# Windowed attention and ELU feed-forward on one core: values loaded and split once per tile of 128 tokens for all heads

## The chip, the cores and the metric

The kernel runs on one core of a Trainium2 chip. The metric is device microseconds of one execution. TensorE does the matmuls (PE in the rows, its weight loads PEld), VectorE (DVE), ScalarE (ACT) and GpSimd (POOL) do the element work, and every transfer is issued by SyncE (SP). Each engine runs its own instructions strictly in program order.

## The reference

```python
# q, k, v: (4, 8, 768, 64) float32; n_sink = 4, window = 128
scores = np.matmul(q, k.transpose(0, 1, 3, 2)) / np.sqrt(64)
keep = (pos[None, :] < n_sink) | ((rel >= 0) & (rel < window))   # rel = query position - key position
a = softmax(np.where(keep, scores, -1e9))
x = np.matmul(a, v)                       # all heads beside each other: (3072, 512)
h = x @ w_in                              # 512 -> 2048
g = np.where(h > 0, h, np.exp(np.minimum(h, 0)) - 1)
out = g @ w_out                           # 2048 -> 512
```

## The kernel before

The 3072 tokens are 24 tiles of 128 (`NT` = 6 to a batch), in nine chunks of 2, 2, 2, 3, 3, 3, 3, 3 and 3 tiles (`SIZES`). For each chunk `attention(c)` makes the four blocks of x (one for each of `NP` = 4 head pairs), and `feed_forward` then goes over 16 blocks of the hidden width, two matmul groups each: `h` (L671, 12 matmuls) and `acc` (L692). The first two chunks take the 16 blocks in two halves (`PARTS`), since the weights, 32 pieces of 512 KB, are still coming in during that time. All operands are carried as a high and a low half (float16, or float32r for keys), made by ACT (the high half) and DVE or POOL (the low one).

A weight piece takes one load, one ACT instruction (L287), three on DVE (L289, L288, L290), then ACT (L436) and POOL (L437). An attention step for a tile and a head pair takes scores on PE (L567 in the first two chunks, L560 and L561 later), a masked minimum on DVE (L586), Exp on ACT (L588), a sum and a reciprocal (L592, L593), the probabilities' two halves (ACT L600, DVE L601), a transposing DMA on SP (L619), the value matmuls on PE (L630, and L635 for the four sink positions), and after a pair's last tile the copy out of PSUM into x (ACT L643, DVE L644). A block of the feed-forward takes ACT (L679, L684), DVE (L681, L682) and POOL (L685).

Values: for each chunk and each head pair, L527 loads a stretch of `vx` that holds, for every key tile of the chunk (the own tiles and the one before the first), 128 columns, and 128 more for the sink rows. ACT makes `vh` of it (L530), DVE `vl` (L531). Where a tile of the chunk lies two or more tiles into its batch, an ACT copy puts low halves of the sink rows into `vh` (L536, 8 partitions). Two raw buffers (`vs`) and two split ones (`vhl`) go round. So there are 36 loads and splits, 384, 512 or 640 columns wide, and 32 sink copies.

The order of all this is set by `Plan`: every step is a task with a cost and its inputs; PE tasks have fixed positions in two or three lines; the others are placed by list scheduling with due times, and the best of eight rounds is written out as each engine's program (`keep_order`). Ring buffers are constraints of the plan (`ring`). A change of tasks therefore changes the order elsewhere too.

Of the kernel before, what the change touches and what calls it, by code (L numbers as in the profile page):

```python
# [20 lines left out]
P = 128  # L21
# [31 lines left out]
RINGS = dict(kqs=2, kq=3, vs=2, vm=1, vhl=2, e=3, st=6, pq=3, pt=6, g=2, gh=3, x=7, wv=4, s=2, po=1, h=2, wu=2, sv=2, wps=1, raw=6)  # L53
# [20 lines left out]
NK_MAX = max(len(key_tiles(c)) for c in CHUNKS)  # L74
# [269 lines left out]
def fast_path(tc, ctx, first, kq, vx, wt, out, nw, flag):  # L344
# [15 lines left out]
    vh = rows("vh", [P, (NK_MAX + 1) * P], F16, RINGS["vhl"])  # L360
    vl = rows("vl", [P, (NK_MAX + 1) * P], F16, RINGS["vhl"])
# [108 lines left out]
    later = []  # L470

    def attention(c):
# [4 lines left out]
        vw = (nk + 1) * P  # L477
        far = any(g % NT >= 2 for g in ts)
# [38 lines left out]

        k = 0
        for p in range(NP):
            kqp = [split_keys(2 * p + e) for e in range(2 if c >= DUP else 1)]  # L520


            st = vs[slot("vs")]
            o = V_OFF[c, p]
            ld = None
            if (c, p) not in first["vs_"]:
                ld = add("SP", 0.4, lambda st=st, o=o: nc.sync.dma_start(st[:, :vw], vx[:, o : o + vw]), lat=dma_us(P * vw * 4))  # L527
            i = slot("vhl")
# [12 lines left out]
            for g in ts:  # L541
# [80 lines left out]
                def values(po=po, vhi=vhi, vlo=vlo, pt=pt, g=g, j=j, nb=nb, t=t):  # L622
# [394 lines left out]
```

## Time and profile before

| what | value |
|---|---|
| median of 3 runs | 658.06 us (657.52 to 658.17) |
| the profiled execution | 658.03 us, its span in the profile 656.2 us |
| PE busy | 611.0 us, 93% of the span |
| DVE, ACT, POOL busy | 458.4, 456.3, 338.8 us |
| mean granted TensorE clock | 0.984 of full speed |

The span is from the first to the last instruction; 1.8 us of the profiled execution lie around it. Busy time is time in which an engine has at least one instruction under way. Idle time of an engine costs only where something at the end waits for it.

### The profile page before, as it was taken

To read this page: it belongs to the slowest core of one execution; us is meant where nothing else is said; L and a number is where in the kernel's file an instruction comes from. 1 tells how busy PE (TensorE), PEld (TensorE's weight loads), DVE (VectorE), ACT (ScalarE), POOL (GpSimd) and SP (SyncE) were. 2 spreads that over 40 slices of the span, in tenths; PEclk is the share of its full clock that TensorE was granted. 3 is DMA by queue.
4 is the path that set the end of the run, shared out by engine and by line. 5 is a ranking of instruction groups with operands and counts; after the bars stand their busy time and mean duration, and the time that the engine had idled before them with its cause. 6 is when DMAs were issued, how large, how long until landed. Compare 5 with 4: busy or idle time off the path is not lost.

```text
span 656.2 us, 13438 instructions
## 1 busy us (share of the span) xinstructions
PE 611.0 (93%) x4449; PEld 370.1 (56%) x4449; DVE 458.4 (70%) x1251; ACT 456.3 (70%) x1340; POOL 338.8 (52%) x497
## 2 busy tenths in 40 slices
PE   3678699789999999999999999999999999999995
PEld 2444466457777665655555565565555556555552
DVE  6999999987677757757676877757686786533222
ACT  4988798887788878767677877766677776523221
POOL 0156878785565767544446656544446654212221
PEclk9998699999999999999999999999999999999998
DMA  7898976765647556445454666454655733211001
GB/s 266 202 284 231 267 213 209 246 171 154 140 126 155 159 151 129 117 116 158 100 147 114 186 135 164 79 157 136 125 140 122 213 91 90 61 42 44 1 0 54
DMA packets 130110, 93.41 MB, mean 142 GB/s; under 512 B 104432, under 2 KB 109552, under 8 KB 130032
## 3 DMA queue, kind: packets, MB, share of 16 engines
q1 hardware_dynamic: 130032, 92.47, 53.2%
q8 instruction: 37, 0.61, 0.4%
q14 instruction: 41, 0.34, 0.2%
HBM read 59.94 MB, written 7.34 MB: 103 GB/s over the span
## 4 chain that ended last, share of the span: by engine, by line
PE 81%; DVE 8%; DMA 3%; ACT 2%; issue 2%; POOL 2%; SPq 0%; DVEq 0%; POOLq 0%; ACTq 0%
PE h L671 35%; PE acc L692 34%; PE po L630 5%; PE s L560 3%; PE s L561 3%; DMA pt<-pq 2%; DVE wv L290 2%; DVE wu L288 1%; DVE pq L601 1%; PE s L567 1%; DVE wu L289 1%; DVE g L681 1%; POOL w L437 1%; ACT e L588 1%; ACT pq L600 1%
## 5 line engine op out<-in xcount | busy, mean ns | idle before, releaser
L671 PE MATMUL h<-x,w 128*128 128x384 f16 (+1 forms) x1728 | 278.1, 312 | 6.1 <-DVE g L682 6.1
L685 POOL TENSOR_TENSOR gl<-g,gh 128x384 f16<-128x384 f32 (+1 forms) x144 | 125.7, 874 | 195.8 <-ACT gh L684 163.2
L671 PEld LDWEIGHTS <-w 128*128 128x128 f16 x1728 | 166.5, 99 | 100.6 <-POOL w L437 4.0
L692 PE MATMUL acc<-w,gh 128*128 128x512 f16 x768 | 194.2, 382 | 0.7 <-ACT gh L684 0.7
L681 DVE TENSOR_SCALAR g<-g 128x384 f32<-128x384 f32 (+1 forms) x144 | 68.2, 474 | 109.1 <-ACT g L679 108.8
L679 ACT ACTIVATE g<-h 128x384 f32<-128x384 f32 (+1 forms) x144 | 65.0, 451 | 84.6 <-PE h L671 77.3
L601 DVE SCALAR_TENSOR_TENSOR pq<-e,st,pq 128x256 f16<-128x256 f32 (+1 forms) x192 | 104.7, 573 | 15.1 <-ACT pq L600 14.5
L692 PE MATMUL acc<-w,gl 128*128 128x512 f16 x384 | 109.3, 380 | 2.4 <-POOL gl L685 2.3
L692 PEld LDWEIGHTS <-gh 128*128 128x128 f16 x768 | 70.0, 98 | 70.9 <-ACT gh L684 1.2
L586 DVE CUSTOM_DVE_ANT_0 e<-s,m 128x264 f32<-128x264 f32 (+1 forms) x192 | 73.5, 404 | 41.5 <-PE s L561 38.0
L588 ACT ACTIVATE e<-e,st 128x264 f32<-128x264 f32 (+1 forms) x192 | 93.4, 487 | 11.5 <-DVE st L586 10.1
L684 ACT ACTIVATE gh<-g 128x384 f16<-128x384 f32 (+1 forms) x144 | 69.2, 481 | 44.6 <-DVE g L682 44.1
L600 ACT ACTIVATE pq<-e,st 128x256 f16<-128x256 f32 (+1 forms) x192 | 84.6, 479 | 10.0 <-DVE st L593 9.4
L507 POOL TENSOR_TENSOR kq<-kqs,kq 128x396 fp32r<-128x396 f32 (+1 forms) x56 | 68.5, 1224 | 37.8 <-ACT kq L503 37.2
L682 DVE SCALAR_TENSOR_TENSOR g<-g,h 128x384 f32<-128x384 f32 (+1 forms) x144 | 72.5, 503 | 1.3
L692 PEld LDWEIGHTS <-gl 128*128 128x128 f16 x384 | 37.5, 98 | 49.0 <-POOL gl L685 4.1
L503 ACT ACTIVATE kq<-kqs 128x780 fp32r<-128x780 f32 (+2 forms) x56 | 48.5, 878 | 17.1 <-PE s L561 15.5
L509 POOL TENSOR_TENSOR kq<-kqs,kq 64x384 fp32r<-64x384 f32 (+1 forms) x56 | 57.0, 1017 | 4.4
L560 PE MATMUL s<-kq 128*128 128x264 f32 x160 | 56.0, 367 | 3.0 <-DVE st L586 2.1
L437 POOL TENSOR_TENSOR w<-wv,w 128x512 f16<-128x512 f32 x32 | 38.8, 1218 | 37.2 <-DVE wu L289 16.6
L630 PE MATMUL po<-pt,vh 128*64 128x128 f16 x704 | 42.1, 230 | 7.7 <-DVE x L644 5.0
L561 PE MATMUL s<-kq 128*128 128x264 f32 x160 | 42.8, 284 | 0.0
(78 smaller groups left out, 620.7 us busy)
## 6 DMA issues: line engine op xcount, KB each, us to landing
raw<-in_wt_dram SPq DMA_DIRECT2D x32, 512.0 KB, 5.2
kqs<-in_kq_dram SPq DMA_DIRECT2D x24, 456.0 KB, 3.4
kqs<-in_kq_dram SPq DMA_DIRECT2D x24, 390.0 KB, 3.3
out_dram<-wv SPq DMA_DIRECT2D x24, 256.0 KB, 2.4
vs<-in_vx_dram SPq DMA_DIRECT2D x20, 256.0 KB, 2.8
vm<-in_vx_dram SPq DMA_DIRECT2D x6, 768.0 KB, 4.8
kqs<-in_kq_dram SPq DMA_DIRECT2D x12, 326.0 KB, 3.4
vs<-in_vx_dram SPq DMA_DIRECT2D x12, 320.0 KB, 3.1
```

What stands on the lines that cost most here:

```text
L560: nc.tensor.matmul(sp[:, :wd], q, hi[:, c0 : c0 + wd], start=True, stop=False)
L586: red = add("DVE", 0.13 + 0.00145 * wd, lambda ee=ee, me=me, sp=sps[e], m=m, wd=wd: nc.vector.tensor_tensor_reduce(ee, sp[:, :wd], m[:, :w ...
L588: ex = add("ACT", 0.48 + 0.00085 * wd, lambda ee=ee, me=me, rs=rs[:, e : e + 1]: nc.scalar.activation(ee, ee, AF.Exp, bias=me, scale=-1.0, ...
L600: a = add("ACT", act_us(nb * P, True), lambda src=src, hi=hi, re=re: nc.scalar.activation(hi, src, AF.Copy, scale=re), deps=[rr])
L601: b = add("DVE", dve_us(nb * P) + 0.1, lambda src=src, hi=hi, lo=lo, re=re: nc.vector.scalar_tensor_tensor(lo, src, re, hi, ALU.mult, ALU. ...
L630: nc.tensor.matmul(po[e * D : (e + 1) * D, oc], vv[:, vo : vo + D], pt[:, (2 * e + part) * nb + i, :], start=new, stop=last)
L671: nc.tensor.matmul(hp[:, :n], win[:, part, d, :], xx[:, :n], start=k == 0, stop=k == 3 * ND - 1)
L681: b = add("DVE", 0.1 + 0.0008 * n, lambda gf=gf: nc.vector.tensor_scalar(gf, gf, -1.0, G_SCALE, ALU.add, ALU.mult), deps=[a])
L682: b = add("DVE", dve_us(n), lambda gf=gf, hp=hp: nc.vector.scalar_tensor_tensor(gf, gf, 0.0, hp[:, :n], ALU.min, ALU.max), deps=[b])
L684: th = add("ACT", act_us(n), lambda gf=gf, gh=gh: nc.scalar.activation(gh[:, :n], gf, AF.Copy), deps=[b])
L685: tl = add("POOL", pool_us(n), lambda gl=gl, gf=gf, gh=gh: nc.gpsimd.tensor_tensor(gl[:, :n], gf, gh[:, :n], ALU.subtract), deps=[th])
L692: nc.tensor.matmul(acc[i], gg[:, i * P : (i + 1) * P], wout[:, part, :], start=f == f0 and k == 0, stop=f == f1 - 1 and k == 2)
```

## The change

Values are laid out in `vx` by token tile: 512 columns for all eight heads, 24 tiles, then one block of 512 columns of sink rows for each of the four batches. `vtile(g)` loads and splits a tile when the plan first asks for it, `sink_rows(b)` does so for a batch's sink rows, whose low halves DVE writes on partitions 64 to 95 in one instruction. All pairs, and the next chunk where it needs the tile again, use the same halves, from a ring of six (`vt`); sink rows have a ring of two (`sk`). There are 24 + 4 loads and 24 + 4 splits, all 512 columns wide, and no ACT copies of sink rows. The value matmuls read other addresses and are otherwise as before. The final range check of the values (L732 to L741) reads the same values in the new layout.

```diff
-RINGS = dict(kqs=2, kq=3, vs=2, vm=1, vhl=2, e=3, ...)
+RINGS = dict(kqs=2, kq=3, vs=2, vm=1, vt=6, sk=2, e=3, ...)
...
+        def vtile(g):
+            if g not in v_of:
+                st, i = vs[slot("vs")], slot("vt")
+                ld = None
+                if g not in first["vs_"]:
+                    ld = add("SP", 0.4, lambda: nc.sync.dma_start(st, vx[:, g * VT : (g + 1) * VT]), lat=dma_us(P * VT * 4))
+                hi, lo, users = vh[i], vl[i], []
+                va = add("ACT", act_us(VT), lambda: nc.scalar.activation(hi, st, AF.Copy, scale=V_SCALE), deps=[ld])
+                vb = add("DVE", 0.13 + 0.00108 * VT, lambda: nc.vector.scalar_tensor_tensor(lo, st, V_SCALE, hi, ALU.mult, ALU.subtract), deps=[va])
+                ring("vs", [ld or va], [va, vb])
+                ring("vt", [va], users)
+                v_of[g] = hi, lo, va, vb, users
+            return v_of[g]
+
+        def sink_rows(b):
+            if b not in sk_of:
+                st, sk, users = vs[slot("vs")], sks[slot("sk")], []
+                o = SINKS + b * VT
+                ld = add("SP", 0.4, lambda: nc.sync.dma_start(st, vx[:, o : o + VT]), lat=dma_us(P * VT * 4))
+                va = add("ACT", act_us(VT), lambda: nc.scalar.activation(sk, st, AF.Copy, scale=V_SCALE), deps=[ld])
+                vb = add("DVE", 0.13 + 0.00108 * VT, lambda: nc.vector.scalar_tensor_tensor(sk[64:96, :], st[64:96, :], V_SCALE, sk[64:96, :], ALU.mult, ALU.subtract), deps=[va])
+                ring("vs", [ld], [va, vb])
+                ring("sk", [va], users)
+                sk_of[b] = sk, vb, users
+            return sk_of[b]
...
-            va = add("ACT", act_us(vw, True), lambda vraw=vraw, vhi=vhi: nc.scalar.activation(vhi, vraw, AF.Copy, scale=V_SCALE), deps=[ld])
-            vb = add("DVE", dve_us(vw) + 0.1, lambda vraw=vraw, vhi=vhi, vlo=vlo: nc.vector.scalar_tensor_tensor(vlo, vraw, V_SCALE, vhi, ALU.mult, ALU.subtract), deps=[va])
-            ring("vs", [ld or va], [va, vb])
-            if far:
-                vb = add("ACT", 0.3, lambda vhi=vhi, vlo=vlo: nc.scalar.activation(vhi[64:72, nk * P :], vlo[64:72, nk * P :], AF.Copy), deps=[vb])
-            ring("vhl", [va], v_users)
...
+                vts = [vtile(g - nb + 1 + i) for i in range(nb)]
+                sk = sink_rows(g // NT) if t >= 2 else None
...
-                val = add("PE", ..., values, deps=[tr, va, vb], ...)
+                val = add("PE", ..., values, deps=[tr, *(d for v in vts for d in v[2:4]), *(sk[1:2] if sk else [])], ...)
```

Of the order that the plan writes, two places on DVE. Line numbers of the change differ: its L597 is L586 of before, L604 is L593, L612 is L601, L287 to L289 are L288 to L290, L661 is L644, L698 and L699 are L681 and L682, and L526 and L539 are the new splits of a tile and of sink rows. `ISA` is the masked minimum (and, with one column, the read of its accumulator).

The first place is in the attention of the second chunk, while weights come in. Before, with `vl_89` the split of the chunk's second head pair:

```order
L288 TENSOR_SCALAR wu_125<-raw_129 128x512
L681 TENSOR_SCALAR g_109<-g_109 128x256
L290 SCALAR_TENSOR_TENSOR wv_121<-acc_171,wu_125 128x512
L682 SCALAR_TENSOR_TENSOR g_109<-g_109,h_164 128x256
L289 TENSOR_SCALAR wu_124<-raw_130 128x512
L288 TENSOR_SCALAR wu_124<-raw_130 128x512
L531 SCALAR_TENSOR_TENSOR vl_89<-vs_73,vh_87 128x512
L290 SCALAR_TENSOR_TENSOR wv_122<-acc_171,wu_124 128x512
L289 TENSOR_SCALAR wu_125<-raw_131 128x512
L288 TENSOR_SCALAR wu_125<-raw_131 128x512
```

In the change, with `vl_95` the split of the chunk's second own tile and `sk_98` its sink rows:

```order
L288 TENSOR_SCALAR wu_134<-raw_138 128x512
L287 TENSOR_SCALAR wu_134<-raw_138 128x512
L539 SCALAR_TENSOR_TENSOR sk_98<-vs_73,sk_98 32x512
L289 SCALAR_TENSOR_TENSOR wv_130<-acc_181,wu_134 128x512
L526 SCALAR_TENSOR_TENSOR vl_95<-vs_72,vh_89 128x512
L698 TENSOR_SCALAR g_119<-g_119 128x256
L288 TENSOR_SCALAR wu_135<-raw_139 128x512
L699 SCALAR_TENSOR_TENSOR g_119<-g_119,h_174 128x256
L287 TENSOR_SCALAR wu_135<-raw_139 128x512
L288 TENSOR_SCALAR wu_134<-raw_140 128x512
```

Before, the splits for the pairs of this chunk stand one by one among the weight pieces, the next two further down; in the change the two rows shown are the last value splits ahead of the sixteenth weight piece's last step, and the chunk's four pairs all need them.

The second place is at the end of the first chunk's attention, from its third `x` to its fourth, after which the feed-forward can begin. Before:

```order
L644 SCALAR_TENSOR_TENSOR x<-po_168,x 128x256
L290 SCALAR_TENSOR_TENSOR wv_123<-acc_171,wu_125 128x512
L586 ISA e_91,st_97<-s_166,m_174 128x264
L586 ISA st_97 128x1
L586 ISA e_91,st_97<-s_167,m_174 128x264
L586 ISA st_97 128x1
L288 TENSOR_SCALAR wu_124<-raw_130 128x512
L289 TENSOR_SCALAR wu_125<-raw_131 128x512
L644 SCALAR_TENSOR_TENSOR x<-po_168,x 128x256
```

In the change:

```order
L661 SCALAR_TENSOR_TENSOR x<-po_178,x 128x256
L289 SCALAR_TENSOR_TENSOR wv_133<-acc_181,wu_135 128x512
L597 ISA e_102,st_108<-s_176,m_184 128x264
L597 ISA st_108 128x1
L597 ISA e_102,st_108<-s_177,m_184 128x264
L597 ISA st_108 128x1
L287 TENSOR_SCALAR wu_134<-raw_140 128x512
L604 RECIPROCAL st_106<-st_106 128x2
L289 SCALAR_TENSOR_TENSOR wv_130<-acc_181,wu_134 128x512
L288 TENSOR_SCALAR wu_135<-raw_141 128x512
L612 SCALAR_TENSOR_TENSOR pq_112<-e_103,st_106,pq_112 128x256
L661 SCALAR_TENSOR_TENSOR x<-po_178,x 128x256
```

Between the third and the fourth `x` stand, in the change, one more weight piece's last step, a reciprocal and a probability half; before, they come behind the fourth `x`.

## Rows read from the trace of the kernel before

**Rows 1.** From the page: busy tenths of PE and DVE in 40 equal slices of 16.4 us, and the granted TensorE clock in tenths of full speed.

```profile
PE   3678699789999999999999999999999999999995
...
DVE  6999999987677757757676877757686786533222
...
PEclk9998699999999999999999999999999999999998
```

**Rows 2.** Busy time by stretch: stretch, its length, then busy us and instructions of PE, PEld, DVE, ACT and POOL, the granted clock, the DMA share, GB/s.

```profile
0.00:20.00 20.00, 7.41 (x30) 4.45 (x30) 14.03 (x66) 11.65 (x39) 2.50 (x18) 1.00 0.74 250
20.00:140.00 120.00, 96.45 (x738) 62.92 (x736) 115.60 (x276) 101.59 (x290) 81.23 (x108) 0.93 0.81 229
140.00:160.00 20.00, 18.49 (x149) 12.73 (x148) 15.26 (x43) 16.18 (x53) 14.92 (x24) 1.00 0.76 207
160.00:640.00 480.00, 480.00 (x3497) 286.11 (x3496) 309.05 (x852) 324.64 (x957) 238.35 (x346) 1.00 0.46 116
```

**Rows 3.** What PE waited for in the first 165 us: us in total, times, longest.

```profile
PE s L567 <- DVE st L586: 9.6, 7, 3.7
PE s L567 <- DMA kqs<-in_kq_dram: 8.3, 3, 6.2
PE h L671 <- DVE g L682: 6.1, 5, 2.2
PE po L630 <- DVE x L644: 5.0, 4, 2.0
PE acc L692 <- POOL gl L685: 2.3, 2, 1.7
```

**Rows 4.** Groups of ACT instructions by line and shape over the whole span: busy us, mean ns of one, idle before.

```profile
L530 ACT ACTIVATE vh<-vs 128x512 f16<-128x512 f32 x20 | 12.4, 619 | 0.0
...
L600 ACT ACTIVATE pq<-e,st 128x128 f16<-128x128 f32 x32 | 11.1, 390 | 1.7 <-DVE st L593 1.7
...
L536 ACT ACTIVATE vh<-vl 8x128 f16<-8x128 f16 x32 | 9.8, 305 | 0.8
...
L530 ACT ACTIVATE vh<-vs 128x384 f16<-128x384 f32 x4 | 2.1, 514 | 4.7 <-DMA vs<-in_vx_dram 4.7
```

**Rows 5.** Groups of DVE instructions between 20 and 140 us: busy us, mean ns of one, idle before.

```profile
L288 DVE TENSOR_SCALAR wu<-raw 128x512 uint16<-128x512 uint16 x30 | 23.6, 788 | 0.0
L290 DVE SCALAR_TENSOR_TENSOR wv<-acc,wu 128x512 int32<-128x512 int32 x30 | 20.4, 680 | 1.0 <-ACT acc L287 0.7 <-DVE wu L289 0.2
...
L601 DVE SCALAR_TENSOR_TENSOR pq<-e,st,pq 128x256 f16<-128x256 f32 x32 | 16.4, 553 | 0.2 <-ACT pq L600 0.2
L681 DVE TENSOR_SCALAR g<-g 128x256 f32<-128x256 f32 x23 | 14.9, 646 | 1.1 <-ACT g L679 1.1
L586 DVE CUSTOM_DVE_ANT_0 e<-s,m 128x264 f32<-128x264 f32 x32 | 12.7, 422 | 1.9 <-PE s L561 1.1 <-PE s L567 0.7
L682 DVE SCALAR_TENSOR_TENSOR g<-g,h 128x256 f32<-128x256 f32 x23 | 9.3, 405 | 0.0
L531 DVE SCALAR_TENSOR_TENSOR vl<-vs,vh 128x512 f16<-128x512 f32 x7 | 6.5, 926 | 0.0
...
L586 DVE DVE_READ_ACCUMULATOR2_ANT st<- 128x1 f32 x34 | 2.7, 79 | 0.0
L593 DVE RECIPROCAL st<-st 128x2 f32<-128x2 f32 x18 | 2.5, 150 | 0.0
...
L531 DVE SCALAR_TENSOR_TENSOR vl<-vs,vh 128x384 f16<-128x384 f32 x2 | 1.1, 553 | 0.0
```

**Rows 6.** The value splits on DVE (L531) by stretch: stretch, its length, busy us (and how many), clock, DMA share, GB/s.

```profile
0.00:20.00 20.00, 1.09 (x2) 1.00 0.74 250
20.00:140.00 120.00, 7.59 (x9) 0.93 0.81 229
```

**Rows 7.** Three rows of the timeline (start, length, engine and instruction): the first chunk's last x on DVE, the first feed-forward matmuls on PE, and the last weight piece's L290 on DVE.

```profile
33.92 0.42 DVE L644 SCALAR_TENSOR_TENSOR x<-po,x 128x256 f16<-128x256 f32 x1
...
34.58 1.68 PE L671 MATMUL h<-x,w 128*128 128x256 f16 x7
...
138.55 0.68 DVE L290 SCALAR_TENSOR_TENSOR wv<-acc,wu 128x512 int32<-128x512 int32 x1
```

**Rows 8.** Five stretches of 5 us, columns as in rows 2.

```profile
45.00:50.00 5.00, 1.32 (x6) 0.85 (x4) 5.00 (x12) 3.91 (x10) 3.15 (x6) 0.80 1.03 290
50.00:55.00 5.00, 5.00 (x20) 2.56 (x18) 4.94 (x14) 4.89 (x14) 4.42 (x6) 0.51 0.82 205
65.00:70.00 5.00, 1.44 (x6) 0.44 (x5) 5.00 (x7) 3.66 (x11) 4.69 (x6) 0.85 0.99 180
70.00:75.00 5.00, 2.53 (x33) 2.12 (x33) 5.00 (x10) 3.08 (x7) 4.92 (x5) 0.50 0.85 290
75.00:80.00 5.00, 5.00 (x24) 3.25 (x23) 5.00 (x13) 4.81 (x16) 4.63 (x9) 0.62 1.01 368
```

**Rows 9.** DMA issues of the values, by size: count, KB each, median us to landing.

```profile
vs<-in_vx_dram SPq DMA_DIRECT2D x20, 256.0 KB, 2.8
...
vs<-in_vx_dram SPq DMA_DIRECT2D x4, 192.0 KB, 4.4
```

**Rows 10.** What SP's queue waited for in the first 165 us, the row of the value loads: us in total, times, longest.

```profile
SPq L527 <- DVE vl L531: 12.6, 6, 3.7
```

**Rows 11.** One line's instructions, L288 on DVE: least, median and longest duration in ns, first and last start in us.

```profile
L288 DVE TENSOR_SCALAR wu<-raw x32: 433/730/1409, 13.8 to 135.3; 128x512 uint16<-128x512 uint16 x32
```

More of the change, by code (lines that the diff above doesn't have):

```diff
@@ L52 @@
 V_AT0 = 5.0
[L53 removed]
+RINGS = dict(kqs=2, kq=3, vs=2, vm=1, vt=6, sk=2, e=3, st=6, pq=3, pt=6, g=2, gh=3, x=7, wv=4, s=2, po=1, h=2, wu=2, sv=2, wps=1, raw=6)
 def key_tiles(ch):
@@ L73 @@
 KL_MAX = max(len(key_tiles(c)) * KW for c in CHUNKS)
-NK_MAX = max(len(key_tiles(c)) for c in CHUNKS)
+VT = NP * P
+SINKS = B * NT * VT
 TOK_MAX = max(SIZES) * P
@@ L620, in attention, with values @@
                 ring("pq", his, [tr])
-                def values(po=po, vhi=vhi, vlo=vlo, pt=pt, g=g, j=j, nb=nb, t=t):
+                vts = [vtile(g - nb + 1 + i) for i in range(nb)]
+                sk = sink_rows(g // NT) if t >= 2 else None
+                def values(po=po, vts=vts, sk=sk, pt=pt, j=j, nb=nb, t=t, p=p):
                     oc = slice(j * P, (j + 1) * P)
                     new, end = j == 0, j == nt - 1
-                    for n, (vv, part) in enumerate(((vhi, 0), (vlo, 0), (vhi, 1))):
+                    for n, (x, part) in enumerate(((0, 0), (1, 0), (0, 1))):
                         for i in range(nb):
@@ L628, in values @@
                             for e in range(2):
-                                vo = kts.index(g - nb + 1 + i) * P + e * D
-                                nc.tensor.matmul(po[e * D : (e + 1) * D, oc], vv[:, vo : vo + D], pt[:, (2 * e + part) * nb + i, :], start=new, stop=last)
+                                vo = p * P + e * D
+                                nc.tensor.matmul(po[e * D : (e + 1) * D, oc], vts[i][x][:, vo : vo + D], pt[:, (2 * e + part) * nb + i, :], start=new, stop=last)
                             new = False
@@ L633, in values @@
                         for e in range(2):
-                            vo = nk * P + e * D
-                            nc.tensor.matmul(po[e * D : (e + 1) * D, oc], vhi[:, vo : vo + D], pt[:, 8, :], start=False, stop=end)
-                val = add("PE", 0.17 * nb + (0.05 if t >= 2 else 0.0) + (0.2 if j == 0 else 0.0), values, deps=[tr, va, vb], pos=at[k - j + nt - 1] + (V_AT0 if c == 0 else V_AT) + 0.01 * j, line=2)
+                            vo = p * P + e * D
+                            nc.tensor.matmul(po[e * D : (e + 1) * D, oc], sk[0][:, vo : vo + D], pt[:, 8, :], start=False, stop=end)
+                val = add("PE", 0.17 * nb + (0.05 if t >= 2 else 0.0) + (0.2 if j == 0 else 0.0), values, deps=[tr, *(d for v in vts for d in v[2:4]), *(sk[1:2] if sk else [])], pos=at[k - j + nt - 1] + (V_AT0 if c == 0 else V_AT) + 0.01 * j, line=2)
                 ring("pt", [tr], [val])
                 vals.append(val)
-                v_users.append(val)
+                for v in vts:
+                    v[4].append(val)
+                if sk:
+                    sk[2].append(val)
                 k += 1
@@ L917, in layouts @@
     kq = np.empty((P, KQ_COLS), q.dtype)
-    vx = np.zeros((P, V_COLS), v.dtype)
+    vx = np.zeros((P, SINKS + B * VT), v.dtype)
+    vx[:, :SINKS].reshape(P, B, NT, H, D)[:] = v.reshape(B, H, NT, P, D).transpose(3, 0, 2, 1, 4)
+    sinks = vx[:, SINKS:].reshape(P, B, H, D)
+    for h in range(H):
+        for r in range(h % 2 * NS, 96, 32):
+            sinks[r : r + NS, :, h] = v[:, h, :NS].transpose(1, 0, 2)
     for c, ch in enumerate(CHUNKS):
         kts = key_tiles(ch)
-        far = [g // NT for g in ch if g % NT >= 2]
         for h in range(H):
@@ L930, in layouts @@
                     o += w
-            o = V_OFF[c, h // 2] + e * D
-            for g in kts:
-                vx[:, o : o + D] = v[g // NT, h, g % NT * P : (g % NT + 1) * P]
-                o += P
-            if far:
-                assert min(far) == max(far)
-                for r in range(e * NS, 96, 32):
-                    vx[r : r + NS, o : o + D] = v[far[0], h, :NS]
     return kq, vx
```

36 lines of the change are left out of this document (12 added, 24 removed).

## The prediction

> **What bounds the kernel now.** The busy tenths come first [rows 1]: PE is full from the tenth slice on to the last but one, and has its holes in the first 160 us, where DVE stands at 9 in nearly every slice. The table by stretch sharpens that [rows 2]. From 160 to 640 us PE is busy for all of the 480 us at full clock, with ACT at 68% and DVE at 64%: nothing that ACT or DVE are spared there can move the end. From 20 to 140 us DVE is busy for 115.6 of 120 us and PE for 96.5. PE idles 12.6 + 23.6 + 1.5 = 37.7 us before 160 us and 7.5 us in the drain at the end, which the change leaves alone. The list of waits says whom PE waits for in that first part [rows 3]: DVE's minima L586 (9.6 us), L682 (6.1 us), the x copies L644 (5.0 us), and first loads of keys and queries (8.3 us, 6.2 of them at the start). So the first 140 us are a queue of DVE work, and the end moves by what that queue gets shorter up to the last weight piece: its L290 starts at 138.55 us [rows 7], and from then on PE has all it needs.
>
> **What the change removes from that queue.** In DVE's program before, 11 value splits stand ahead of the last weight piece's L290: the four pairs of the first chunk (384 columns) and seven of 512. They take 1.09 us up to 20 us and 7.61 us from 20 to 140 us, 8.7 us in all [rows 6]. In the changed program 7 stand there, all 512 columns wide: the tiles of the first three chunks, six, and the first batch's sink rows. At the 0.926 us that a 512-column split costs in this stretch [rows 5] they take 6.5 us. **DVE: 8.7 - 6.5 = 2.2 us less.**
>
> One of the seven, the sink rows, works on 32 partitions, and no row of before has that shape on DVE. The nearest rows are on ACT: a copy on 8 partitions takes 305 ns, one of as many columns on 128 partitions takes 390 ns [rows 4], so 16 times fewer partitions bought 22%. Its lower bound is then 0.78 x 0.926 = 0.72 us, its upper bound 0.926 us; I take the upper one, and the difference, 0.2 us, is in the range.
>
> The Trainium skill speaks against a cheap sink row too ("VectorE: DVE Perf Modes", section "Why tensor_reduce can't reduce along partition axis"): DVE streams along the free dimension and each partition is a lane of its own, so 32 lanes would take as long as 128. By it the sum stays 2.2 us; if cost went with the partitions the op would be 0.23 us and the sum 2.9 us. No run here shows the DVE instruction itself yet.
>
> **What the same change does on the other engines up to there.** On ACT, 12 splits (4 x 0.514 + 8 x 0.619 us) and 6 sink copies (0.305 us each) stand ahead of the last piece's L436, together 8.8 us [rows 4]; after, 9 splits of 0.619 us, 5.6 us: 3.2 us less. I count that at nothing: ACT is busy for 101.6 of those 120 us, less than DVE [rows 2], so DVE's queue covers it; without that cover it would be worth up to its 3.2 us. Of loads, 4 x 192 + 8 x 256 KB go out ahead of the last weight piece before, 9 x 256 KB after [rows 9]: 512 KB less, 2.3 us of transfers at the 229 GB/s of that stretch [rows 2], counted at nothing for the same reason, since PE's waits name a load only for the first keys and queries [rows 3]. The first values are 256 KB instead of 192, ahead of the second keys and queries: 64 KB at 250 GB/s are 0.26 us, which could cost at the very start and is left in the range. PE does the same matmuls. After 160 us, 13 more splits and their sink copies fall away or move, under PE's 480 full us: nothing.
>
> **What is moved.** The plan writes a new order, and the same queue is dealt out otherwise. Up to the last weight piece's L290, DVE of the change also has 2 more minima with their accumulator reads (0.422 + 0.079 us each), 4 more L601 (0.553 us) and one more L681 and L682 (1.05 us) in front of it: 4.3 us of other work pulled ahead, so that this L290 comes 2.1 us of DVE work later; the 24th L682, which the last block before the saturated stretch needs, comes earlier by 3.5 us (no last L290 ahead of it, 0.68; the splits, 2.2; two L601 fewer, 1.1; but one minimum more, 0.5). Work done earlier needn't be done later, so I let these cancel and keep the 2.2 us. In the second chunk all four pairs now hang on the two splits `sk` and `vl` of DVE's order, first place: two minima, two L601 and wider splits stand more ahead of them than ahead of the first pair's split before (1.0 + 1.1 + 1.5 = 3.6 us of DVE), but the later three pairs find theirs done, where before each had its own among the weight pieces. SP waited 12.6 us, in six times, for DVE to free a raw buffer of values [rows 10], with weight loads, keys and transposes queued behind. There are still two such buffers; the change asks for them 9 times instead of 12 up to the last weight piece, and its fifth and sixth tile's loads stand right behind each other on SP, behind these same two splits. I give that no price of its own: it is part of the range.
>
> **Sum.** The profiled execution took 658.03 us, its span 656.2, and the median of the runs is 658.06. 658.0 - 2.2 = **655.8 us**. A difference under 0.2%, 1.3 us, is about what a measurement of this kernel cannot tell from none.
>
> **Rivals.**
>
> *The front is slower (22%).* The feed-forward begins when the first chunk's fourth x is copied: L644 at 33.92 us, the first `h` matmul at 34.58 us [rows 7]. In the change the fourth L644 has ahead of it 2 more minima (1.0 us with their reads), one more L601 (0.55), one more L593 (0.15) and one more L290 (0.68), and three splits of 512 columns instead of four of 384, by rows 5 3 x 0.926 instead of 4 x 0.55, 0.6 us more: 3.0 us. If that delay stays, because PE then eats through its blocks no faster than the weight pieces come, the end moves back by 3.0 us, and the 2.2 us taken from DVE turn into idle time of DVE: 661.0 us. It decides if the first `h` starts after about 37 us and the last L290 no earlier than now. Against it: DVE's later queue is shorter by the same work, and between 40 and 140 us PE waits for DVE and not the other way round.
>
> *No difference (20%).* DVE is full, but others are nearly so, and its instructions aren't of one length: an L288 takes between 0.43 and 1.41 us [rows 11], 0.788 on average in this stretch [rows 5], while POOL is busy for 81 of 120 us [rows 2]. If POOL's pace (the low halves of weights and keys) sets the length, 2.2 us less on DVE become waits of DVE for ACT and POOL: 658.0 us, give or take 1. For it speaks that POOL's work, one instruction for each weight piece and two for each head's keys, stays as it is; against it that PE's waits name POOL for only 2.3 us [rows 3].
>
> *A larger gain (10%).* Between 50 and 55 us and between 70 and 80 us the granted clock is 0.51, 0.50 and 0.62 [rows 8], that is mostly at the 1.2 GHz level; ahead of each PE was busy for only 1.3 and 1.4 of 5 us. Where PE is busy throughout at such a clock, full clock would give back 5 x 0.49 = 2.5 us and 5 x 0.38 = 1.9 us, and in the third stretch 2.53 x 0.5 = 1.3 us, 5.7 us in all. In those idle stretches DVE's value splits are dearest. If the order without them closes the holes, the clock stays up; since DVE then binds again, I count half: 658.0 - 2.2 - 2.8 = 653.0 us.
>
> **How the numbers follow.** The forecast has 48%, with a range of its own from 653.5 us (ACT's 3.2 us count in part) to 657.5 us (the 0.26 us at the start, and most of what was pulled ahead, cost). Some 8 of the 48 lie within 1.3 us of now. Faster by over 0.2%: 40 + 10 = 50%. Within: 20 + 8 = 28%. Slower: 22%. The range from 652.5 to 660.5 us takes in the larger gain's middle and most of the slower front; I leave out 2 in 10 at its ends.
>
> **What would show it.** In the profile of the changed kernel: 24 + 4 splits on DVE and ACT with 512 columns; a sink split on 32 partitions at 0.7 to 0.93 us; seven splits on DVE before the last L290, 6.5 us; that L290 at 136 to 139 us; PE without idle time from about 158 us; the sum of PE's idle time before 160 us near 35.5 us instead of 37.7. The forecast is wrong if the first `h` starts after 37 us, if stretches at half clock grow or shrink by more than 3 us, or if DVE shows idle time of more than 3 us more between 20 and 140 us.

## The result, and the profile after

| | kernel before | changed kernel |
|---|---|---|
| median of the runs, us | 657.79 (657.40 to 658.17, 4 runs) | 664.10 (663.50 to 664.97, 4 runs) |
| ratio after to before | | 1.0098, 95% interval 1.0082 to 1.0114 |
| profiled execution, its span, us | 658.03, 656.2 | 663.87, 662.0 |

The changed kernel is 6.3 us slower; the forecast was 2.2 us faster, and the time lies 3.6 us above the range. From its page, the lines of [rows 1], with the busy totals:

```profile
PE 616.2 (93%) x4449; PEld 371.3 (56%) x4449; DVE 453.9 (69%) x1243; ACT 442.4 (67%) x1300; POOL 335.8 (51%) x497
...
PE   3777689889999989999999999999999999999996
...
DVE  6979879998777756667666776668677776524223
...
PEclk9997779999999989999999999999999999999999
```

The busy time by stretch, columns as in [rows 2]:

```profile
0.00:20.00 20.00, 6.60 (x28) 4.09 (x29) 14.00 (x66) 11.27 (x34) 1.71 (x18) 1.00 0.78 264
20.00:140.00 120.00, 97.48 (x718) 61.80 (x718) 107.97 (x269) 97.47 (x283) 80.34 (x106) 0.91 0.78 221
140.00:160.00 20.00, 19.11 (x153) 13.22 (x152) 17.77 (x49) 15.87 (x51) 16.34 (x27) 1.00 0.83 201
160.00:640.00 480.00, 477.35 (x3476) 284.61 (x3475) 308.18 (x842) 313.69 (x924) 233.78 (x346) 1.00 0.48 113
```

DVE is busy for 108.0 us between 20 and 140 us, 7.6 less than before (in part the relief on splits, in part work that now lies behind 140 us, the last weight piece's last step among it), and ACT has 4.1 and (from 160 to 640 us) 11.0 us less. Yet PE's idle time before 160 us only fell from 37.7 to 36.8 us, and from 160 to 640 us PE now has a hole of 2.7 us where it had none. The waits of PE, columns as in [rows 3], up to 165 us and then from 165 to 650 us:

```profile
PE po L644 <- DMA pt<-pq: 9.4, 9, 2.3
PE s L578 <- DMA kqs<-in_kq_dram: 7.5, 2, 6.4
PE s L578 <- DVE st L597: 5.0, 5, 2.7
PE h L688 <- POOL w L437: 4.2, 5, 1.2
PE s L571 <- DVE st L597: 3.1, 4, 1.6
PE h L688 <- DVE g L699: 2.7, 2, 1.6
```

```profile
PE po L644 <- DMA pt<-pq: 2.2, 1, 2.2
PE s L571 <- DVE st L597: 0.4, 1, 0.4
```

The waits have changed names: the minima (L597 here) and L699 are down from [rows 3], POOL's low halves of weights (L437) are new, and transposed probabilities `pt` are the largest now. In the same 165 us of the kernel before they were:

```profile
PE po L630 <- DMA pt<-pq: 1.5, 3, 0.6
```

The rows that answer to [rows 7], with that one late wait of PE as third row (start, length, instruction, idle time ahead and what ended it):

```profile
37.74 0.42 DVE L661 SCALAR_TENSOR_TENSOR x<-po,x 128x256 f16<-128x256 f32 x1 [1.94 <-ACT x L660]
```

```profile
37.22 4.68 PE L688 MATMUL h<-x,w 128*128 128x256 f16 x24
```

```profile
237.95 0.30 PE L644 MATMUL po<-pt,vh 128*64 128x128 f16 x4 [2.25 <-DMA pt<-pq]
```

```profile
144.54 0.68 DVE L289 SCALAR_TENSOR_TENSOR wv<-acc,wu 128x512 int32<-128x512 int32 x1
```

The fourth x is copied at 37.74 us instead of 33.92, the first `h` matmul starts at 37.22 us instead of 34.58 (its first nine matmuls read the other three x), and the last weight piece's L289 starts at 144.54 us instead of 138.55. Stretches at half clock, columns as in [rows 8]:

```profile
55.00:60.00 5.00, 2.66 (x15) 1.59 (x12) 4.72 (x9) 3.14 (x8) 4.75 (x5) 0.50 1.03 386
70.00:75.00 5.00, 3.95 (x25) 2.34 (x21) 4.73 (x13) 2.22 (x7) 4.39 (x7) 0.50 0.98 358
85.00:90.00 5.00, 3.42 (x16) 2.64 (x17) 4.29 (x12) 3.05 (x7) 4.63 (x10) 0.55 0.89 316
235.00:240.00 5.00, 2.75 (x46) 1.64 (x41) 2.30 (x7) 2.18 (x7) 1.51 (x4) 0.91 1.18 217
240.00:245.00 5.00, 5.00 (x24) 2.99 (x23) 1.80 (x6) 2.90 (x8) 2.52 (x3) 0.75 0.19 54
```

Where the time went is read from when each feed-forward block (12 matmuls of L671, L688 after) starts. Differences to the profiled execution of the kernel before, in us, worked out from the timelines, for this kernel and those of the experiments. Each row is of one profiled execution, which need not be the median one: mid_later's took 669.4 us, its slowest. From block 49 on all kernels have the same matmuls behind them (old_nudged two more at block 49); at blocks 1 to 32 some are up to 34 matmuls of attention ahead, the changed kernel 20 at block 13:

| kernel | median, us | block 1 | 8 | 13 | 32 | 49 | 53 | 144 |
|---|---|---|---|---|---|---|---|---|
| changed kernel | 664.1 | +2.6 | -1.7 | +5.1 | +3.4 | +3.1 | +7.1 | +7.0 |
| mid_later | 666.1 | +2.7 | -1.0 | +4.2 | +2.7 | +2.3 | +8.0 | +12.0 |
| front_later | 664.7 | +2.7 | -0.8 | +6.0 | +5.2 | +5.0 | +6.8 | +6.6 |
| both_later | 667.6 | +2.7 | 0.0 | +5.6 | +4.8 | +4.7 | +6.8 | +8.6 |
| jit12 | 659.9 | +2.1 | -0.1 | +2.7 | +2.3 | +2.2 | +2.2 | +2.5 |
| jit12_nudged | 666.7 | +3.0 | +1.4 | +8.6 | +6.9 | +8.3 | +8.7 | +9.3 |
| jit12_nudged2 | 660.8 | +1.5 | +1.4 | +4.1 | +2.8 | +2.8 | +2.8 | +3.0 |
| new_work_old_order | 662.3 | +1.3 | -0.6 | +4.5 | +4.2 | +4.2 | +4.1 | +4.0 |
| old_work_new_order | 669.7 | +3.4 | +1.4 | +6.3 | +9.3 | +10.6 | +12.6 | +12.5 |
| old_nudged | 664.8 | +2.5 | -1.0 | +2.2 | +5.6 | +7.5 | +7.2 | +7.2 |
| old_nudged2 | 661.5 | -0.2 | -1.8 | +3.4 | +4.3 | +4.5 | +4.8 | +4.8 |
| new_nudged | 664.2 | +3.7 | +0.5 | +6.6 | +6.0 | +6.4 | +6.4 | +6.3 |
| new_nudged2 | 663.2 | +3.1 | -3.0 | -0.3 | +2.4 | +2.9 | +5.6 | +5.5 |
| new_start_old_rest | 660.4 | +1.7 | -1.6 | +3.9 | +2.3 | +1.8 | +1.8 | +1.7 |
| old_start_new_rest | 670.7 | +1.3 | +0.2 | +0.3 | +1.1 | +8.4 | +12.6 | +12.5 |
| old_front_new_rest | 667.7 | +0.9 | +1.2 | +6.7 | +7.5 | +8.3 | +9.7 | +9.5 |
| old_front_held_rest | 660.3 | +1.3 | -0.8 | +2.4 | +2.3 | +2.0 | +2.0 | +2.8 |

In the changed kernel the start costs 3.1 us up to block 49, the wait at 237.95 us and the half clock behind it 4.0 us (block 49 to 53), and a drain that is shorter by 1.2 us gives some back: 5.8 us of span. Beside the experiments the kernel before took 657.7 to 658.6 us (medians), single executions 655.6 to 660.7.

### The profile page after: what moved, and what is told of

Read it like the earlier page. It is cut to its first block, busy times and chain, and to the rows that moved or that the text cites. A ratio compares the mean times of both kernels' runs of the same rounds, so it can differ in the third digit from the quotient of the medians.

```text
span 662.0 us, 13340 instructions
## 1 busy us (share of the span) xinstructions
PE 616.2 (93%) x4449; PEld 371.3 (56%) x4449; DVE 453.9 (69%) x1243; ACT 442.4 (67%) x1300; POOL 335.8 (51%) x497
## 4 chain that ended last, share of the span: by engine, by line
PE 64%; DMA 1%; issue 1%; POOL 0%; DVE 0%
PE acc L709 28%; PE h L688 28%; PE po L644 3%; PE s L571 2%; PE s L572 2%; DMA pt<-pq 1%; PE po L649 0%; POOL gl L702 0%; DVE wv L734 0%
## 5 line engine op out<-in xcount | busy, mean ns | idle before, releaser
L688 PE MATMUL h<-x,w 128*128 128x384 f16 (+1 forms) x1728 | 280.7, 313 | 7.9 <-POOL w L437 4.2
L688 PEld LDWEIGHTS <-w 128*128 128x128 f16 x1728 | 166.9, 99 | 102.7 <-POOL w L437 7.2
L698 DVE TENSOR_SCALAR g<-g 128x384 f32<-128x384 f32 (+1 forms) x144 | 65.7, 457 | 111.5 <-ACT g L696 110.9
L612 DVE SCALAR_TENSOR_TENSOR pq<-e,st,pq 128x256 f16<-128x256 f32 (+1 forms) x192 | 112.9, 616 | 12.6 <-ACT pq L611 11.6
L597 DVE CUSTOM_DVE_ANT_0 e<-s,m 128x264 f32<-128x264 f32 (+1 forms) x192 | 72.9, 403 | 48.7 <-PE s L572 42.4
L611 ACT ACTIVATE pq<-e,st 128x256 f16<-128x256 f32 (+1 forms) x192 | 85.7, 480 | 13.6 <-DVE st L604 13.3
L506 POOL TENSOR_TENSOR kq<-kqs,kq 128x396 fp32r<-128x396 f32 (+1 forms) x56 | 66.9, 1194 | 29.3 <-ACT kq L502 28.9
L699 DVE SCALAR_TENSOR_TENSOR g<-g,h 128x384 f32<-128x384 f32 (+1 forms) x144 | 72.7, 505 | 1.5
L437 POOL TENSOR_TENSOR w<-wv,w 128x512 f16<-128x512 f32 x32 | 39.7, 1245 | 45.0 <-ACT w L436 44.5
L571 PE MATMUL s<-kq 128*128 128x264 f32 x160 | 56.6, 371 | 5.0 <-DVE st L597 3.5
L644 PE MATMUL po<-pt,vh 128*64 128x128 f16 x704 | 43.1, 230 | 12.6 <-DMA pt<-pq 11.7
L644 PEld LDWEIGHTS <-vh 128*64 128x64 f16 x704 | 30.6, 114 | 28.6 <-issue 20.5
```

The lines of the kernel that those rows point to most:

```text
L506: nc.gpsimd.tensor_tensor(buf[:, KQ_MAX : KQ_MAX + n] if c >= DUP else buf[:, kw : 2 * kw], raw[:, :n], hi[:, :n].bitcast(F32), ALU.subtract)
L571: nc.tensor.matmul(sp[:, :wd], q, hi[:, c0 : c0 + wd], start=True, stop=False)
L597: red = add("DVE", 0.13 + 0.00145 * wd, lambda ee=ee, me=me, sp=sps[e], m=m, wd=wd: nc.vector.tensor_tensor_reduce(ee, sp[:, :wd], m[:, :w ...
L611: a = add("ACT", act_us(nb * P, True), lambda src=src, hi=hi, re=re: nc.scalar.activation(hi, src, AF.Copy, scale=re), deps=[rr])
L612: b = add("DVE", dve_us(nb * P) + 0.1, lambda src=src, hi=hi, lo=lo, re=re: nc.vector.scalar_tensor_tensor(lo, src, re, hi, ALU.mult, ALU. ...
L644: nc.tensor.matmul(po[e * D : (e + 1) * D, oc], vts[i][x][:, vo : vo + D], pt[:, (2 * e + part) * nb + i, :], start=new, stop=last)
```

## The experiments

**Moving the new splits.** The first suspicion fell on the new splits of value tiles. Two of them stand among ACT's rows ahead of that late wait (L525, here of tiles 12 and 13, which are first needed some 70 us later), in front of an L611, the instruction that normalises the probabilities for the transpose:

```profile
229.47 0.62 ACT L525 ACTIVATE vh<-vs 128x512 f16<-128x512 f32 x1
...
232.02 0.62 ACT L525 ACTIVATE vh<-vs 128x512 f16<-128x512 f32 x1
...
234.08 0.49 ACT L611 ACTIVATE pq<-e,st 128x256 f16<-128x256 f32 x1
```

This L611 was taken for that of the step whose transpose PE waits for. In mid_later these two splits go behind the step (the loop in the diff), in front_later those of tile 2 and of the first sink rows go behind the first chunk's attention (the line ahead of it), in both_later both.

```diff
     tasks = plan.order()
+    moves = {}
+    moves.update(dict.fromkeys((*v_of[2][2:4], sk_of[0][3]), 24.5))
+    for g in (12, 13):
+        moves.update(dict.fromkeys(v_of[g][2:4], 10.0))
+    tasks = put_later(tasks, moves)
...
+def put_later(order, moves):
+    s = {}
+    for t in order:
+        s[t] = max([t.start + moves.get(t, 0.0), *(s[d] + 1e-6 for d in t.deps)])
+    return sorted(order, key=lambda t: (s[t], t.n))
```

> The changed kernel with one piece of its order changed: after the plan is made, the ACT and DVE splits of value tiles 12 and 13 (needed first around 305 us) are put 10 planned us later, so that they no longer stand between the two exponentials and the normalising instructions of the third attention step of chunk 4. Work and everything else are the same. Theory 1 (early splits stand in the way of an urgent attention step): the 2.25 us wait of PE for the transpose at 235.7 us and the half-clock stretch behind it go, 664.1 - 4.4 = about 659.7 us; the first h block stays at 37.2 us. Theory 2 (the plan as a whole fell out worse, the two splits are only where it shows): the wait comes back within the next steps, the time stays within 1 us of 664.1. Theory 3 (the front alone costs the time): no change, 664.1 us.

> The changed kernel with the ACT and DVE splits of value tile 2 and the ACT split of batch 0's sink rows (first needed at about 52 us) put 24.5 planned us later, out of the first chunk's attention; the load of tile 3 goes with them, since it reuses the buffer. Theory 1: the first h block starts at about 34.6 us again in place of 37.2 and the time falls by up to 2.6 us, to 661.5-662.5; the stall at 235.7 us stays. Theory 2: the start of the first h changes by less than 1 us and the time goes anywhere within 2 us. Theory 3: the whole loss goes, 658 us.

> Both moves in one kernel. Theory 1: the two add, 664.1 - 4.4 - 2.6 = about 657.1 us, the time of the kernel before within 1 us. Theory 2: not the sum of the two single moves, 660-665 us. Theory 3: as the front move alone, 658 us.

Measured: 666.12 us (664.05 to 669.36; ratio to before 1.0111, 1.0079 to 1.0142), 664.69 (1.0103, 1.0072 to 1.0134) and 667.64 (1.0167, 1.0123 to 1.0210). Theory 1 falls: none is faster than the changed kernel. With the splits out of the way PE waits for the same transpose, and longer, and then for minima (mid_later: the row of the timeline, and one of the waits from 165 us on):

```profile
237.86 0.42 PE L644 MATMUL po<-pt,vh 128*64 128x128 f16 x4 [2.89 <-DMA pt<-pq]
```

```profile
PE s L571 <- DVE st L597: 2.4, 2, 2.0
```

PE had arrived 0.7 us earlier (block 49 already started that much earlier) and the transpose came 0.1 us earlier. With the first chunk's splits gone the first `h` still starts 2.7 us late. That is nearest to theory 2, which had the time too low by 1 us; theory 3 (the front alone) was not put to the test, since front_later left the first `h` where it was.

The timeline of the changed kernel shows that the suspicion had the wrong step. PE's wait up to 237.95 us ended when a transpose landed (237.91 us) that SP had issued at 231.26. ACT's share of its probabilities was done at 225.91 us and DVE's at 230.54, before either engine began the first of these two splits (229.47 and 230.93). The L611 at 234.08 belongs to the next step, whose transpose went out at 236.66, landed at 240.17 and was needed at 257.32. What stands right ahead of the late one is in SP's queue, a load of keys and two output stores, and behind them SP was held by the issue for 3.53 us:

```profile
228.31 1.28 SPq L630 DMA_TRANSPOSE pt<-pq  x1
229.70 0.51 SPq L501 DMA_DIRECT2D kqs<-in_kq_dram  x1
230.26 0.90 SPq L735 DMA_DIRECT2D out_dram<-wv  x2
231.26 3.53 SPq L630 DMA_TRANSPOSE pt<-pq  x1
```

The time from issue to landing, first of the transpose at 231.26 alone, then of the one at 228.31 alone (count, us):

```profile
pt<-pq SPq DMA_TRANSPOSE x1, 6.6
```

```profile
pt<-pq SPq DMA_TRANSPOSE x1, 2.8
```

mid_later, front_later and both_later have the same load and stores right ahead of this transpose, and it landed 7.3, 6.0 and 6.3 us after its issue.

**Making the plan hold the splits back.** In jit12 the planner itself may not start a split more than 12 planned us ahead of need, so the whole order is made anew.

```diff
+AHEAD_V = 12.0
...
             else:
+                ready[t] = max(ready[t], t.due - t.ahead if t.ahead else 0.0)
                 for e in t.ways:
...
                 ring("vt", [va], users)
+                va.ahead = vb.ahead = AHEAD_V
```

> The changed kernel in which the plan may start a split of a value tile or of sink rows no earlier than 12 planned us before its due time (due minus 12 is put in as the earliest start); the rest of the plan is made anew around that. Theory 1: no split stands in the way of a step that is due earlier by much, so neither the front nor the stall at 235 us is there, and the change's saving on DVE and ACT shows: 655-657.5 us. Theory 2: a new plan, so a new time anywhere between 655 and 666 us, with a wait of over 1.5 us for a transpose somewhere after 160 us. Theory 3: 656-658 us if the first h starts before 35 us, 661 or more if it starts after 37.

Measured: 659.92 us (659.33 to 663.71, 8 runs), ratio 1.0031 (1.0007 to 1.0056). No long wait of PE after 165 us:

```profile
PE s L575 <- DVE st L601: 0.4, 1, 0.4
PE po L648 <- DMA pt<-pq: 0.3, 1, 0.3
```

4 us better than the changed kernel, but above theory 1's 657.5, and with the first `h` at 36.6 us between theory 3's two cases; the time fits theory 2, though its wait did not come. It leaves open whether the hold did it or merely a new order.

**Crossing work and order.** All tasks but the value splits and their loads (3,028) are the same in both kernels. Each kernel's work was put in the other's order from a table of ranks:

```diff
     tasks = plan.order()
+    tasks = in_order_of_other(tasks, plan.tasks)
...
+def in_order_of_other(order, made):
+    s, rank = {}, dict(zip(made, RANK))
+    for t in order:
+        s[t] = max([rank[t], *(s[d] + 1e-4 for d in t.deps)])
+    return sorted(order, key=lambda t: (s[t], t.n))
+RANK = [
...
+]
```

> The changed kernel's work in the order of the kernel before: each of the 3,028 planned tasks that have nothing to do with the values stands on its engine in exactly the order that it had in the kernel before; the 28 new splits (24 tiles, 4 times sink rows) and their loads stand where the kernel before had splits and loads of value pieces. Theory A (the order that the plan fell into costs the time): 658.6 us or less, 655-658, first h at 34.6 us, no wait of PE for a transpose after 160 us. Theory B (the new work itself costs it: splits per tile come before they are needed, the 32-partition split of sink rows): 661 us or more, with the first h at 36 us or later.

> The reverse: the kernel before, its 36 splits per chunk and head pair included, with the 3,028 other tasks in the order of the changed kernel (two neighbouring steps of PE stand the other way round). Each split of values stands behind the same task of its engine as in the kernel before, so that the conversions of tiles 12 and 13 in the middle of a chunk's first pair are not there. Theory A: as slow as the changed kernel or slower, 662-668 us, with a wait of PE for a transpose of over 1.5 us at about 235 us. Theory B: 657-660 us, as the kernel before.

| | order of before | order of the changed kernel |
|---|---|---|
| old work | 657.7 | 669.7 (1.0190, 1.0147 to 1.0232) |
| new work | 662.3 (1.0065, 1.0043 to 1.0087) | 664.1 |

The new order costs the old work 12.0 us and the new work 1.8; the new work costs 4.6 us in the old order and gains 5.6 in the new one. The new order costs both; the work has no sign of its own. Theory A has the new order right, if too low with its 662 to 668: PE waits for transposes there without a single tile split (three times, 3.0 us):

```profile
PE po L630 <- DMA pt<-pq: 3.0, 3, 1.8
```

The other cell is theory B's by its time, and nearly so by the first `h` (35.9 us for 36 or later): the new work in the old order keeps PE free of waits from 165 us on, but isn't as fast as before. Of its 4.2 us, 5.1 come between blocks 8 and 13 (the blocks ahead had gained a little): a `pt` that PE waits 2.63 us for, up to 85.28 us, and a half clock behind it. That this needn't be so with this work and order is shown by a later run with both the same up to 185 planned us (old_start_new_rest), whose block 13 is only 0.3 us late. The same two stretches, first of new_work_old_order, then of old_start_new_rest, and each one's transposes between 72 and 90 us (count, median us to landing):

```profile
80.00:85.00 5.00, 2.17 (x12) 1.07 (x10) 3.21 (x11) 3.38 (x10) 2.90 (x4) 0.98 1.30 171
85.00:90.00 5.00, 4.72 (x40) 3.60 (x40) 2.44 (x7) 2.09 (x8) 0.99 (x1) 0.50 0.56 177
```

```profile
80.00:85.00 5.00, 3.99 (x39) 2.58 (x38) 3.44 (x12) 3.15 (x10) 2.88 (x4) 1.00 1.14 196
85.00:90.00 5.00, 5.00 (x48) 3.73 (x47) 5.00 (x14) 4.27 (x15) 3.09 (x6) 1.00 0.32 89
```

```profile
pt<-pq SPq DMA_TRANSPOSE x2, 7.1
```

```profile
pt<-pq SPq DMA_TRANSPOSE x2, 5.6
```

Where the transposes landed 1.5 us later, PE waited longer and the clock fell behind it; where they landed earlier, it stayed up. One order can go either way.

**Redrawing the order with the same work.** One planning number, which costs nothing on the chip, is changed by 0.02: behind DVE in the first nudge, behind ACT in the second.

```diff
-    HOP = {"PE": 0.15, "ACT": 0.08, "DVE": 0.08, "POOL": 0.2, "SP": 0.0}
+    HOP = {"PE": 0.15, "ACT": 0.08, "DVE": 0.10, "POOL": 0.2, "SP": 0.0}
```

> The changed kernel with one number of the planner changed (the planned hop behind a DVE instruction 0.10 in place of 0.08 planned us), the same work: a plan made anew, with another order. Theory A: the time differs from 664 us by more than 2 us either way, most likely lower, 657-664, since the order of the changed kernel is one of many draws and a poor one. Theory B: 662-666 us with the first h at about 37 us and a wait for a transpose in the 230s.

> The kernel before with the same number of the planner changed, the same work as before, another order. Theory A: up to several us slower than the kernel before, 659-667 us, since the order of the kernel before is a good draw. Theory B: within 1.5 us of 658.

> The changed kernel with the same number of the planner changed. Theory A: 657-667 us, from the same spread as the old work's new orders. Theory B: 663 us or more, as the two orders of the changed kernel that ran so far.

> The kernel before with another number of the planner changed (the planned hop behind an ACT instruction 0.10 in place of 0.08), same work, another order. Theory A (orders are draws that differ by several us; the kernel before had a good one): 659-667 us. Theory B (the first nudge was unlucky, 658 us is what the old work takes): within 1.5 us of 658.

> The changed kernel with splits held to 12 planned us before they are due, and the planned hop behind a DVE instruction 0.10. Theory A (a draw): 656-667 us. Theory B (the hold is what mends the changed kernel): 658-661 us again, with no wait for a transpose of over 1.5 us after 160 us.

> The same hold with the planned hop behind an ACT instruction 0.10. Theory A: 656-667 us. Theory B: 658-661 us again, with no wait for a transpose of over 1.5 us after 160 us.

Measured: the old work in two new orders 664.75 us (1.0111, 1.0093 to 1.0129) and 661.48 (1.0046, 1.0004 to 1.0089); the changed kernel's work 664.24 (1.0092, 1.0072 to 1.0112) and 663.24 (1.0092, 1.0040 to 1.0144); with the hold 666.71 (1.0141, 1.0096 to 1.0187) and 660.81 (1.0051, 1.0034 to 1.0068). Both orders of the old work fall where theory A put them and theory B didn't. Of the new work, new_nudged came out level with the changed kernel, against theory A, but without the wait in the 230s that theory B named; new_nudged2 fits both. The hold is no cure by itself: jit12_nudged took 666.7, as only theory A allowed. So three orders of the old work give 658, 661 and 665, three of the new work 663 to 664, three with the hold 660 to 667. The order of the kernel before is the best of its three; the spread of orders is larger than anything that the work could be seen to be worth.

**Dividing the order.** The new work in one order up to a planned time, in the other from there on (the same table of ranks).

> The changed kernel's work: all tasks that the changed kernel planned before 185 us in its own order, all others behind them in the order of the kernel before. If the wait at 235.7 us comes from the order from there on, it is gone: first h at 37.2 us, block 45 some 2.7 us later than in the kernel before, and so are block 53 and the end: about 660.5 us. If it comes from the new work or from what the start leaves behind, 664 us.

> The reverse: the start, up to 185 planned us, in the order of the kernel before (as in the run of the new work in the old order, which lost 4.2 us up to block 13), and the rest in the changed kernel's own order. If the wait belongs to that order, it comes on top: 662.3 + 4.4 = 666-667 us, with a wait for a transpose of 1.5 us or more at about 237 us. If not, 662-663 us.

> The changed kernel's work with the first 38 planned us in the order of the kernel before and all the rest in its own order. If the late first h block is the order of the front, h starts at 36 us or before, as in the new work in the old order (35.9). If the time lost there carries through, the end is 1.3-2.6 us earlier than in the changed kernel, 661.5-663 us; if the next waits and half-clock stretches take it back, 664 us.

> The first 38 planned us in the order of the kernel before, the rest in the order that the plan found with splits held to 12 us before they are due (659.9 us with its own front, whose first h block was 2.1 us later than in the kernel before). If the front's time carries through, about 0.8 us less than that order with its own front, 659.1 us, and no wait for a transpose of over 1.5 us after 160 us; if new waits and half clocks take it, 660-664 us.

Measured: 660.36 us (1.0029, 1.0008 to 1.0050), 670.67 (1.0192, 1.0143 to 1.0241), 667.73 (1.0133, 1.0074 to 1.0192) and 660.25 (1.0032, 1.0014 to 1.0049). PE's waits from 165 us on, first of new_start_old_rest, then of old_start_new_rest:

```profile
PE po L644 <- DMA pt<-pq: 0.4, 1, 0.4
```

```profile
PE s L571 <- DVE st L597: 4.1, 2, 3.7
PE po L644 <- DMA pt<-pq: 3.1, 2, 2.6
```

The late wait belongs to the order from 185 us on: take it away and it goes, as expected (660.36 for about 660.5); put it behind the old start and it comes back, 4.2 us between blocks 49 and 53. The 3.7 us wait for a minimum (blocks 32 to 49) is a cost of joining the two orders that wasn't expected. What the order brings with it is again that transpose. Of the 18 kernels with a profile, seven issue it within 1.6 us behind a load of keys and two output stores (the changed kernel, the three with moved splits, old_work_new_order, old_start_new_rest and new_nudged2): it landed 5.2 to 7.3 us after its issue, and PE waited 1.6 to 2.9 us for it. In the other eleven, the kernel before among them, it landed after 2.9 to 4.9 us, and PE waited for it in one (old_front_new_rest, 1.2 us).

The front's order does set the first `h` (+0.9 and +1.3 instead of +2.6 and +2.1; with the changed kernel's own start, new_start_old_rest has +1.7), but nothing of it reaches the end: old_front_new_rest ends later than the changed kernel, old_front_held_rest level with jit12. No order tried makes the new work faster than the kernel before.

## Why the prediction was wrong, point by point

**"So the first 140 us are a queue of DVE work, and the end moves by what that queue gets shorter"** is the step that failed. The queue did get shorter: up to the last weight piece's last step DVE was busy for 126.5 us instead of 128.2 (worked out from the timelines). That step came 6.0 us later all the same, since DVE was idle for 18.0 us ahead of it instead of 10.4. Between 20 and 140 us it waited for PE's scores (L597), for ACT's part of the feed-forward (L698) and for ACT's copies of x (L661), columns as in [rows 5], where the first two had 1.9 and 1.1 us:

```profile
L597 DVE CUSTOM_DVE_ANT_0 e<-s,m 128x264 f32<-128x264 f32 x33 | 13.0, 421 | 3.4 <-PE s L572 1.9 <-PE s L578 1.5
L698 DVE TENSOR_SCALAR g<-g 128x256 f32<-128x256 f32 x23 | 12.1, 527 | 3.9 <-ACT g L696 3.5
...
L661 DVE SCALAR_TENSOR_TENSOR x<-po,x 128x256 f16<-128x256 f32 x9 | 3.7, 413 | 2.4 <-ACT x L660 2.4
```

PE in turn waited for transposes, 9.4 us instead of 1.5 in the first 165 us; SP's queue, which issues them, was the term that the prediction gave "no price of its own". DVE was the limit of one order, and the new order had another.

**"Nothing that ACT or DVE are spared there can move the end"** was taken for "nothing can". PE's 480 full us from 160 us on [rows 2] are a property of one order too; the redrawn one had a hole there, 4.0 us with its half clock.

**DVE's 2.2 us** were there: the seven splits ahead of the last L289 take 6.2 us (6.5 forecast; the 7.61 us of before are 7.59 in [rows 6], which changes nothing), and the sink rows on 32 partitions took 0.684 us, one row of the groups between 20 and 140 us (columns as in [rows 5]):

```profile
L526 DVE SCALAR_TENSOR_TENSOR vl<-vs,vh 128x512 f16<-128x512 f32 x3 | 3.4, 1149 | 0.0
...
L539 DVE SCALAR_TENSOR_TENSOR sk<-vs,sk 32x512 f16<-32x512 f32 x1 | 0.7, 684 | 0.0
```

That is what a tile split on 128 partitions takes in the quiet start of this run (0.69, 0.67 and 0.68 us), so the Trainium skill ("VectorE: DVE Perf Modes", section "Why tensor_reduce can't reduce along partition axis") agrees with the trace. The forecast's bounds, 0.72 to 0.926, missed it because both were taken from the mean of the busy stretch, where some splits are slow (1.15 us on average for the three here) and this one was not. **ACT's relief and the loads** were rightly counted at nothing.

**"So I let these cancel"** went wrong with it. The fourth x came 3.8 us later. From 22 us up to it DVE ran 10 minima instead of 7 and finished 3 weight pieces instead of 2, which is 1.6 us more of busy time; the other 2.2 us DVE stood idle, 1.94 of them right ahead of that x, for ACT's copy and so for PE's values. One transpose ahead of them went out at 29.74 us instead of 28.26 and took 5.0 us to land instead of 3.3. DVE's relief became idle time, 12.0 instead of 4.4 us between 20 and 140 us, more than the 3 us that were named as proof against the forecast.

**The rival "the front is slower"**, held at 22%, seems to be borne out: both of its conditions held, the first `h` after 37 us (37.22) and the last weight piece no earlier (144.54 instead of 138.55), and its 661.0 us are near the 658.0 + 3.1 measured up to block 49. But its mechanism, a delay that stays, did not come, so the number is luck. By block 8 the changed kernel was 1.7 us ahead of the kernel before. It lost time anew behind that: between blocks 8 and 10 PE waited 1.1 us for a transpose, 1.4 for a reciprocal and 1.6 for a minimum, and the clock was granted at 0.55 from 85 to 90 us, after PE had been busy for 2.5 of the 5 us before. Nor do the first `h` and block 49 go together in the other kernels: -0.2 and +4.5 in old_nudged2, +0.9 and +8.3 in old_front_new_rest, +3.1 and +2.9 in new_nudged2.

**The rest, 4.0 us, had no rival.** All rivals asked what the change does to a fixed kind of order, while the plan draws the order. The range was built from terms of the change and left out that term, which is larger than any that it priced: three planned orders of one and the same old work span 7 us.

**Not settled:** whether the load and the stores ahead of the late transpose make it late by themselves. They stand there in every kernel that waits long for it, but for the shorter wait of old_front_new_rest; none was moved by itself. The two splits are excluded, the order from 185 us on is shown. What makes the start slow, 3.1 us up to block 49, is not shown either: with the order of before the new work lost 4.2 us there in one execution, and 1.1 us up to block 32 in another. So it isn't settled what the new work is worth in a fixed order (in the old one its median is 4.6 us above the kernel before), nor over many orders: the three planned orders of the old work average 661 us, the three of the new work 664, too few to tell.

## What to carry to other kernels

Where a planner or a list scheduler writes the order, taking work away redraws the whole order, and the draw can be worth more than the work: redraw it a few times with the old work (a planning constant moved by a little) before any gain or loss is laid to the change, and run the new work in the old order as well. An instruction that stands in the way of an urgent one is a suspect, not a cause; move it alone and look whether the wait ends earlier. Before that, find the transfer that ended the wait by its landing time, and read what stands ahead of that one in its queue. A saturated stretch proves nothing about the next order of the same work.

## What the hardware showed that was not expected

One order with one work took two courses: in two executions with the same instructions in the same order up to 185 planned us, the two transposes around 80 us landed after 7.1 or 5.6 us (medians), PE waited 2.63 or 1.00 us, the clock was granted at 0.50 or 1.00 from 85 to 90 us, and block 13 started 4.2 us apart.

A transpose right behind bulk transfers landed late. From 165 us on, over the 18 kernels, 443 transposes had no load or store issued by SP in the 5 us ahead of them and landed 2.8 us after their issue (median; 2.3 to 5.1), the seven within 1.6 us behind a load of keys and two output stores after 5.2 to 7.3.

DVE can slow beside POOL. Three L612 in a row, while POOL made low halves of keys and of g, and one alone just after (DVE, then POOL, of the changed kernel):

```profile
226.05 3.23 DVE L612 SCALAR_TENSOR_TENSOR pq<-e,st,pq 128x256 f16<-128x256 f32 x3
...
230.07 0.47 DVE L612 SCALAR_TENSOR_TENSOR pq<-e,st,pq 128x256 f16<-128x256 f32 x1
```

```profile
225.46 1.33 POOL L506 TENSOR_TENSOR kq<-kqs,kq 128x528 fp32r<-128x528 f32 x1
226.87 1.07 POOL L508 TENSOR_TENSOR kq<-kqs,kq 64x384 fp32r<-64x384 f32 x1
228.02 0.98 POOL L702 TENSOR_TENSOR gl<-g,gh 128x384 f16<-128x384 f32 x1
```

3.23 us for three, 1.08 each, and 0.47 for the one. The Trainium skill ("Trainium Architecture — The Big Picture", section "What this means for kernel authors") names DVE and GpSimd as the two engines that contend for a port pair of SBUF; these rows agree, with a factor of 2.3. Not every such pair is slow: of the 160 L612 of this shape, the 39 with no POOL instruction beside them took 0.47 to 0.49 us, the 47 with one beside them for over nine tenths of their time 0.46 to 1.59. The planner counts with one duration for all, so a step planned close to need beside POOL can come late. The third of the slow three and the one behind them make the low halves for the late transpose of the changed kernel; what they cost there was not tried.
